# Value-stationary attention products in four column tiles, block transposes for their results, earlier requests for the last weights, no barrier behind the projections, and a redone order of units

## Chip, cores and metric

One core of one Trainium2 chip. The metric is device time in microseconds (us) for one execution; lower is better.

Terms: PE is TensorE, which multiplies matrices; DVE is VectorE, ACT is ScalarE, POOL is GpSimd. TensorE writes its results to PSUM, which this kernel uses in eight banks; an eviction is the copy of a result out of PSUM by DVE or ACT, after which the bank is free again. Filler is work that no waiting step needs at once, put where TensorE would idle.

## The reference, cut to what matters

The result is `g * a + (1 - g) * b`, with two independent attentions over one input of 2048 rows by 512 columns.

**A** is recurrent. The 2048 rows are 64 segments of 32 rows. Each segment gets 8 memory rows in front, and those are the first 8 output rows of the segment before:

```python
for s in range(n_seg):                       # 64, strictly one after another
    h = concatenate([mem, xs], axis=1)       # 8 + 32 rows of 512
    q, k, v = h @ Wq, h @ Wk, h @ Wv         # 32 heads of 128
    p = softmax(mask(q @ k.T * scale))
    o = (p @ v) @ Wo                         # 40 rows of 512
    mem = o[:, :M, :]                        # needed by the next segment
    outs.append(o[:, M:, :])
```

**B** is a causal attention in 4 blocks of 512 rows, 32 heads of 16, with a linear-attention memory carried from block to block. Its softmax-weighted values are divided by their sum, scaled by `1 - g`, and from the second block on a memory part `(phi(q) @ M) / (phi(q) @ z) * g` is added.

A is a loop of 64 dependent steps. B is independent of A, and the kernel uses it to fill TensorE's idle time between A's steps.

## The kernel before

Each engine gets a fixed list of operations; semaphore waits come from recorded reads and writes. A segment of A is a list of named units, one list for each segment number modulo 4. This is the second one:

```python
# K0x..V1y: projections of half 0/1 of the heads; k0,q0,v0: their evictions; TQ,TK: transposes
# S: scores, X: exp, M: row sums, L: reciprocal, N: normalise (n: the "left" columns)
# PV0/PL0, PV1/PL1: values times probabilities, main and left part, of half 0 and 1
# E0a,E0b,E1a,E1b: evictions of those;  W..: product with Wo;  H,l: split into high and low;  F: fold
# Fc,Ff,Fe: filler for the next four segments;  hm,ax: evictions of memory rows and of the other rows;  oL: left outputs set aside
#  bS,bE,bP: B's scores, exp, PV;  bT: B's result chain
"""Q0x K0x bE Q0y K0y K1x q0 TQ0 V0x Q1x Q1y k0 TK0 q1 S0 K1y X0 V0y TQ1 M0 k1 bS TK1 L0 bP V1x n0 S1 V1y X1 M1 Fc N0 bE v0 L1 v1
   PV0 PL0 Fc N1 E0b bP E0a Fe n1 Fe PV1 PL1 W0a W0b E1b E1a bT W1b W1a H0 H1 l0 bS l1 Ff bP F0 Ff oL hm0 ax0 F1 hm1 bE ax1 Fe Fe"""
A_ENG = dict(E0a="dve", E0b="act", ..., H0="act", Q0="dve", Q1="dve", ...)   # who evicts what
```

B's PV has the probabilities stationary and moves 17 columns (16 values and a one for the sum):

```python
for e, kc, q, col in blocks:
    for x in range(2):
        pe.matmul(pb[ob][:, o:o+17], pt[:, x, col:col+128], V[:, kc, 17*h:17*(h+1)], ...)
# chain: DVE reads the sums, takes reciprocals, multiplies; TensorE turns the result with 4 transposes
```

Before the segments lie B's projections, the loads of the weights, and a barrier:

```python
bar = []
for e in ("pe", "act", "dve", "gp"):
    o_ = P.ops[e][-1]; o_.post = True; bar.append(o_)
P.extra = bar
```

The softmax here doesn't subtract the row's maximum and nothing guards it: scores larger than these inputs give would overflow.

## Time and profile before

| | before |
|---|---|
| median, 3 runs (range) | 996.97 us (995.89 to 999.29) |
| profiled span | 994.1 us |
| TensorE / DVE / ACT busy | 93 % / 62 % / 58 % |
| end of segment 0 / of segment 63 | 107.0 / 985.6 us |
| mean segment | 13.95 us |

A segment's end is the end of the second copy of its memory rows (`hT`) out of PSUM.

**How segments are accounted below.** From the trace, from the end of segment 4 to the end of segment 56, I take the start-to-start time of every two neighbouring TensorE groups. A fixed time for each kind of group and 90 to 113 ns for each change of tile mode (the values that undisturbed neighbours show) count as work; the rest is waiting. Gaps inside a group count as waits "inside groups". Before, a segment of 14.10 us has 12.95 us work and 1.15 us waits. (The prediction has 12.4 and 1.7: it took the fast tenth of every pair of groups as work, which is stricter. I compare differences only.)

### The profile page before, as it was taken

How to read it: one execution, taken by the hardware profiler on the slowest of the kernel's cores; microseconds unless marked ns; L12 is line 12 of the kernel's file. 1: busy time of each engine (PE TensorE's matmuls, PEld its weight loads, DVE VectorE, ACT ScalarE, POOL GpSimd, SP SyncE). 2: the span in 40 equal slices, each digit the busy share in tenths (PEclk: the TensorE clock that was granted, in tenths of full speed). 3: DMA queues.
4: the chain of work that ended last, by engine and by line, in shares of the span. 5: the costliest groups of instructions: out<-in, count | busy, mean ns of one | idle time of the engine just before them, and what ended most of it. 6: DMA issues, size and time to landing. Idle time of an engine off the chain costs nothing.

```text
span 994.1 us, 57017 instructions
## 1 busy us (share of the span) xinstructions
PE 925.5 (93%) x25669; PEld 546.3 (55%) x25669; DVE 619.1 (62%) x1536; ACT 579.9 (58%) x1195; POOL 259.8 (26%) x672
## 2 busy tenths in 40 slices
PE   7986899999999999999999999999999999999986
PEld 4433455555555555555555555555556555555554
DVE  4664456666566666666665766666666667667664
ACT  4454456566666656656666566656656656665443
POOL 6201122222222222322232322232222222322110
PEclk9998899999999999999999999999999999999999
DMA  9897000000000111010001111010011101000010
GB/s 299 282 382 232 19 12 17 12 18 17 17 21 21 44 41 29 21 26 16 22 19 31 43 34 33 20 27 14 20 32 36 36 21 36 21 21 4 25 41 18
DMA packets 65899, 51.71 MB, mean 52 GB/s; under 512 B 34288, under 2 KB 64120, under 8 KB 64120
## 3 DMA queue, kind: packets, MB, share of 16 engines
q1 hardware_dynamic: 65656, 48.06, 16.5%
q8 instruction: 202, 3.31, 1.4%
q14 instruction: 41, 0.34, 0.1%
HBM read 33.47 MB, written 14.57 MB: 48 GB/s over the span
## 4 chain that ended last, share of the span: by engine, by line
PE 81%; ACT 6%; DVE 5%; DMA 3%; issue 3%; SPq 0%; ACTq 0%; POOL 0%; DVEq 0%; POOLq 0%
PE ps L890 40%; PE ps L943 14%; PE ps L716 4%; PE ps L769 3%; PE ps L964 3%; PE ps L591 2%; PE ps L1167 2%; PE ps L1111 2%; PE ps L1137 2%; PE ps L566 2%; DMA scr_pQd<-stgp 2%; PE ps L1104 1%; PE ps L1031 1%; DMA Wo_sb<-in_A_Wo_dram 1%; PE ps L1107 1%
## 5 line engine op out<-in xcount | busy, mean ns | idle before, releaser
L738 POOL TENSOR_SCALAR_AFFINE_SELECT PT<-PT 128x256 bf16<-128x256 bf16 (+1 forms) x224 | 98.3, 439 | 262.9 <-ACT PT L730 200.3
L730 ACT ACTIVATE PT<-ps 128x1024 bf16<-128x1024 f32 x160 | 163.1, 1020 | 5.6 <-PE ps L716 5.4
L320 ACT ACTIVATE KN_sb<-ps 128x512 bf16<-128x512 f32 x128 | 96.9, 757 | 101.3 <-PE ps L890 100.2
L890 PE MATMUL ps<-Wv_sb,hT 128*32 128x512 bf16 x2048 | 147.5, 380 | 0.3 <-ACT KN_sb L320 0.3
L943 PE MATMUL ps<-Wo_sb,OT_sb 128*32 128x256 bf16 x4096 | 139.2, 276 | 7.7 <-DMA Wo_sb<-in_A_Wo_dram 3.3
L890 PE MATMUL ps<-Wk_sb,hT 128*32 128x512 bf16 x2048 | 146.2, 382 | 0.1
L890 PE MATMUL ps<-Wq_sb,hT 128*32 128x512 bf16 x2048 | 142.2, 382 | 0.0
L322 DVE CAST QN_sb<-ps 128x512 bf16<-128x512 f32 x128 | 96.1, 751 | 62.5 <-PE ps L890 61.4
L943 PEld LDWEIGHTS ps<-Wo_sb,OT_sb 128*32 128x32 bf16 x4096 | 99.1, 97 | 26.0 <-issue 9.6
L1157 POOL TENSOR_TENSOR Pn_sb<-P_sb,R_sb 128x64 bf16<-128x64 bf16 x128 | 47.8, 373 | 233.8 <-ACT R_sb L1147 212.7
L902 DVE STREAM_TRANSPOSE KT_sb<-KN_sb 128x256 f32<-128x256 f32 x128 | 57.0, 446 | 65.5 <-ACT KN_sb L320 64.5
L322 DVE CAST V_sb<-ps 128x512 bf16<-128x512 f32 x128 | 87.1, 680 | 11.0 <-PE ps L890 10.2
L320 ACT ACTIVATE OT_sb<-ps 128x320 bf16<-128x320 f32 x192 | 76.2, 433 | 28.6 <-PE ps L1180 28.3
L1120 ACT ACTIVATE P_sb<-ps 128x224 bf16<-128x224 f32 x128 | 45.7, 357 | 76.5 <-PE ps L1111 64.7
L320 ACT ACTIVATE WH<-ps 128x256 bf16<-128x256 f32 x128 | 42.5, 381 | 76.3 <-PE ps L943 61.2
L954 DVE TENSOR_TENSOR WL<-ps,WH 128x256 bf16<-128x256 f32 x128 | 48.7, 420 | 52.8 <-ACT WH L320 45.8
L890 PEld LDWEIGHTS ps<-Wq_sb,hT 128*32 128x32 bf16 x2048 | 47.6, 96 | 53.0 <-DVE hT L322 12.2
L890 PEld LDWEIGHTS ps<-Wk_sb,hT 128*32 128x32 bf16 x2048 | 50.6, 96 | 43.3 <-ACT KN_sb L320 1.5
L320 ACT ACTIVATE LN_sb<-ps 128x512 bf16<-128x512 f32 (+1 forms) x80 | 46.2, 604 | 35.1 <-PE ps L890 18.7
L890 PEld LDWEIGHTS ps<-Wv_sb,hT 128*32 128x32 bf16 x2048 | 48.9, 96 | 30.1 <-ACT KN_sb L320 0.7
L769 PEld LDWEIGHTS ps<-Vj,PT 128*128 128x128 bf16 x1280 | 43.3, 96 | 35.9 <-issue 27.0
L716 PE MATMUL ps<-QTj,KTj 32*128 32x384 bf16 (+3 forms) x512 | 62.1, 301 | 0.1
(129 smaller groups left out, 1515.5 us busy)
## 6 DMA issues: line engine op xcount, KB each, us to landing
Wk_sb<-in_A_Wk_dram SPq DMA_DIRECT2D x4, 1024.0 KB, 6.9
Wq_sb<-in_A_Wq_dram SPq DMA_DIRECT2D x4, 1024.0 KB, 7.4
Wv_sb<-in_A_Wv_dram SPq DMA_DIRECT2D x4, 1024.0 KB, 9.2
Wo_sb<-in_A_Wo_dram SPq DMA_DIRECT2D x4, 1024.0 KB, 10.7
scr_vd<-V SPq DMA_DIRECT2D x16, 136.0 KB, 5.9
Vj<-scr_vd SPq DMA_DIRECT2D x32, 68.0 KB, 2.6
Wo_sb<-in_A_x_dram SPq DMA_DIRECT2D x4, 512.0 KB, 7.5
scr_kTd<-stgk SPq DMA_DIRECT2D x16, 128.0 KB, 6.6
```

What stands on the lines that cost most here:

```text
L320: P.op("act", lambda a: a.activation(dst, src, ACT.Copy), reads=[v.rbank[k] for k in bks], writes=dres, name=name)
L322: P.op("dve", lambda d: d.tensor_copy(dst, src), reads=[v.rbank[k] for k in bks], writes=dres, name=name)
L716: ins = pe.matmul(v.pb[bks[x]][:, o:o + w], KT[e][r, 128 * kc:128 * (kc + 1)], QT[r, q0:q0 + w], start=True, stop=True, tile_position=(r.s ...
L730: P.op("act", lambda a: a.activation(pt[:, :, :], v.ps[:, bks[0]:bks[1] + 1, :], ACT.Exp, scale=v.SCALE_B), reads=[v.rbank[b] for b in bks ...
L738: P.op("gp", lambda g, mv=mv: g.affine_select(mv, mv, [[0, mv.shape[1]], [1, 128]], ALU.is_ge, 0.0, base=0, channel_multiplier=-1), reads= ...
L769: ins = pe.matmul(v.pb[ob][:, o:o + 17], pt[:, x, col:col + 128], V[:, kc, 17 * h:17 * (h + 1)], start=first, stop=True, skip_group_check= ...
L890: ins = pe.matmul(pb[bk][SEG * j:SEG * (j + 1), :], lhs(c), cols(w, j) if split else w[:, 512 * j:512 * (j + 1)], start=(c == 0), stop=(c ...
L902: P.op("dve", lambda d: d.transpose(to, src), reads=reads, writes=writes, name=name)
L943: ins = pe.matmul(pb[bks[hf]][SEG * j:SEG * (j + 1), 0:HD], lhs(4 * k + j), Wo_sb[:, 4 * k + j, HD * hf:HD * (hf + 1)], start=(first and k ...
L954: P.op("dve", lambda d: d.tensor_tensor(lo[:, c], pb[bks[hf]][:, 0:HD], hi[:, c], ALU.subtract), reads=[rbank[bks[hf]], Rs(res[0][hf])], w ...
L1120: P.op("act", lambda a: a.activation(P_sb[:, b, :], pb[bk][:, 0:224], ACT.Exp, scale=SCALE), reads=[rbank[bk]], writes=[Rs("P%d" % b)], na ...
L1157: P.op(ENG["n"], lambda d: d.tensor_tensor(left(Pn_sb), left(P_sb), grp04(R_sb[:, b, :]), ALU.mult), reads=[Rs("P%d" % b), Rs("R%d" % b)], ...
```

## The change

Intent: take TensorE time out of B and out of the changes of tile mode, take the start's barrier away, and use ACT's spare time.

- B's PV has the values stationary, in four column tiles of 32, with 256 or 128 moving columns: 768 matmuls instead of 1280. Results come out transposed; DVE turns them with 32x32 block transposes (56 from PSUM, 16 of the joined result), and TensorE's 64 transposes go.
- B's chain and its memory part become two pieces. The unit orders and the engine choices are redone: Q0 of A goes from DVE to ACT, H0 from ACT to DVE.
- The barrier goes. Each tile that lies over memory of the projections waits for what used it. Wo is requested inside the projections.

```diff
-            for e, kc, q, col in blocks:
-                for x in range(2):
-                    ins = pe.matmul(v.pb[ob][:, o:o + 17], pt[:, x, col:col + 128], V[:, kc, 17 * h:17 * (h + 1)], ...)
+            for kc, q0, w, o in self.PIECES[k]:
+                for j in range(4):
+                    ins = pe.matmul(v.pb[ob][32 * j:32 * j + 32, q0:q0 + w], V[:, kc, G, 17 * j:17 * j + 32],
+                                    pt[:, j // 2, 256 * (j % 2) + o:256 * (j % 2) + o + w], start=(k == 0), stop=True, ...)
         if k == 4:
             self.late.append(lambda: self.chain(job, G, ob))
+            if sb:
+                self.late.append(lambda: self.memory(job, G))
+    def turned(self, bk, name):
+        P.op("dve", lambda d: d.transpose(v.oTt[:, :, :], src), reads=[v.rbank[bk]], writes=[Rs("oTt")], name=name)
...
-        if len(weights) > 4 and n % 5 == 0:
+        if weights and (n % 5 == 0 or n > 55 and n % 2):
             weights.pop(0)()
-    bar = []
-    for e in ("pe", "act", "dve", "gp"):
-        o_ = P.ops[e][-1]
-        o_.post = True
-        bar.append(o_)
-    P.extra = bar
...
     # the second of the four unit orders
-    Q0x K0x bE Q0y K0y K1x q0 TQ0 V0x Q1x Q1y k0 TK0 q1 S0 K1y X0 V0y TQ1 M0 k1 bS TK1 L0 bP V1x n0 S1 V1y X1 M1 Fc N0 bE v0 L1 v1 PV0 PL0
-    Fc N1 E0b bP E0a Fe n1 Fe PV1 PL1 W0a W0b E1b E1a bT W1b W1a H0 H1 l0 bS l1 Ff bP F0 Ff oL hm0 ax0 F1 hm1 bE ax1 Fe Fe""",
+    bS Fe K0x K0y Q0x Q0y K1x k0 bP Q1x Q1y TK0 K1y q0 TQ0 bE S0 q1 k1 V0x bS TQ1 TK1 V0y V1x S1 X0 bE V1y X1 M0 v0 L0 M1 L1 n0 v1 Fc bP
+    Ff N0 PV0 PL0 N1 E0a Fe PV1 n1 bT PL1 E0b E1a W0a E1b oL W0b W1a W1b H1 bP bS H0 Fc Ff l0 l1 F0 hm0 ax0 bE F1 hm1 Fe ax1 Ff Fe""",
-A_ENG = dict(..., H0="act", KL0="dve", Q0="dve", VL0="dve", ...)
+A_ENG = dict(..., H0="dve", KL0="act", Q0="act", VL0="act", ...)
```

A's probabilities are now normalised in place.

## The prediction

> **What bounds the kernel.** TensorE. The profile page gives PE 93% busy, 81% of the chain that ended last, DVE 62%, ACT 58%. The granted clock is 1.00 from 200 to 800 us. From the end of one segment's memory rows to the next it takes 14.1 us (mean of segments 5 to 55; timeline, the 128x16 casts to hT). Adding start-to-start times of matmul groups (their fast tenth as base) over 200 to 900 us, about 12.4 us of a segment is work and about 1.7 us waits, spread over many places (Wo to fold, V projection, second PV half). Before the segments lies a start of 79 us: projections end at 70.6, the first segment projection starts at 79.2 (barrier; POOL xL), then PE waits for Wo (landed about 101.8); segment 0 ends at 107.
>
> **What changes on PE.** B's PV takes 1280 matmuls of 17 columns, 25 to 28 ns each: about 33 us. [...] After: 768 matmuls in four column tiles, 640 of 256 columns and 128 of 128. The Wo matmuls have that shape and take 28 ns each (111 ns for four), so estimated 18 us: saves 15.
>
> Tile shape changes cost too. [...] Here eight projection matmuls take 432 ns before another column-tiled group and 553 before B's PV; score pieces take 320 instead of 216. Each switch thus costs about 0.09 to 0.12 us. Counting both programs' PE order I find about 743 switches before, 616 after: saves 12 to 13 us. The 64 result transposes (3.6 us) go to DVE; the memory products grow from 3.4 to 5.2. Scores stay (same columns). Sum: about 28 us less PE work, 0.45 us a segment.
>
> **Other engines.** DVE gains 56 block transposes, estimated 0.7 us each (128x64 takes 0.25, 128x256 0.45): 40 us; it loses Q0 (48 us) and two left evictions (22), gets H0 (27): about level. ACT gains about 45 us and stays under 67%. POOL loses about 20 us of masks. None becomes the bound.
>
> **Start.** Without the barrier the first segment projection needs only xL (over V17, whose last stores land about 73) and weights: I expect it near 73 to 75. Wo requested inside the projections should land near 90 instead of 102. Segment 0 should end near 96: 8 to 13 us gained. All of it is on the critical path.
>
> **How much is realised.** Where PE is latency-bound, less filler means longer waits: the last segments, with roughly 2.5 us less work, get only 1.6 us shorter (12.5 against 14.1). So I count 65 to 105% of 28 us (the order was redone): 18 to 30, plus 8 to 13 at the start. Predicted 958 us, range 941 to 974; faster by over 2%: 0.91, within: 0.08, slower: 0.01.
>
> **What would show it.** B's PV groups of four at about 110 ns with no gain in time of the projection before; segments near 13.6 us; first segment projection at 73 to 75; no PE wait for Wo above 1 us; PE busy under 900 us; DVE about 620, ACT about 625.
>
> **What would make it wrong.** DVE in order: a block transpose plus its chain (about 1.6 us) before H0 holds up the fold, so waits grow over 2 us a segment. Wo's 4 MB ahead of the last stores delays stage buffers that lie under the segment's tiles. Or the new order removes more waits than I credit, and the time falls under 941.

B's matmuls of 17 columns start 25 ns apart (median). About 28 us less TensorE work, 0.45 us a segment, rests on the times that stand beside it (25 to 28 ns for a matmul of 17 columns, 28 ns for one of Wo's, 432 ns against 553 and 216 against 320 for a change of tile shape).

## More of the kernel before

The two halves of the heads interleave: while half 0 goes through its softmax (S0, X0, M0, L0, N0), TensorE projects half 1 (K1, V1). Each half of PV takes four of the eight PSUM banks:

```python
def pv_main(b):
    bks = held[b] = B.pair() + B.pair()          # four banks
    for i in range(4):
        for j in range(4):                       # 16 matmuls, one bank per 32 rows
            pe.matmul(pb[bks[j]][:, L*i:L*(i+1)], V_sb[...], Pn_sb[...], tile_position=(SEG*j, 0), ...)
# ... ot_ev(b, half): one eviction per two banks, on DVE or ACT, gives them back
```

The profile page of the kernel before: the busy time of each engine with its instruction count, the queue that carries instructions, and the chain of work that ended last.

```profile
PE 925.5 (93%) x25669; PEld 546.3 (55%) x25669; DVE 619.1 (62%) x1536; ACT 579.9 (58%) x1195; POOL 259.8 (26%) x672
...
q8 instruction: 202, 3.31, 1.4%
...
PE 81%; ACT 6%; DVE 5%; DMA 3%; issue 3%; SPq 0%; ACTq 0%; POOL 0%; DVEq 0%; POOLq 0%
```

TensorE is the bound: 81 % of the chain. The second line says 202 packets and 3.31 MB of instructions, that is 16.4 KB each.

The groups of TensorE instructions of the kernel before, by shape: line, operation, output<-inputs, tile mode and shape, count, busy us and mean ns, then TensorE's idle time just before them and what ended it. They are the product with Wo, the PV of A and the fold.

```profile
L943 PE MATMUL ps<-Wo_sb,OT_sb 128*32 128x256 bf16 x4096 | 139.2, 276 | 7.7 <-DMA Wo_sb<-in_A_Wo_dram 3.3 <-issue 3.2 <-DVE LN_sb L954 0.7
...
L1167 PE MATMUL ps<-Pn_sb,V_sb 32*128 32x40 bf16 x2048 | 35.3, 178 | 14.8 <-ACT OT_sb L320 8.8 <-DVE OT_sb L322 2.8 <-DVE Pn_sb L1151 1.9
...
L964 PE MATMUL ps<-fold,WH 128*128 128x32 bf16 x256 | 29.3, 177 | 12.7 <-DVE WL L954 11.3 <-issue 0.3
```

The waits are small and spread. "issue" is time in which TensorE waited for nothing that the profile shows.

The timeline of TensorE in one segment of the kernel before, from the row sums of the second half to the product with Wo (start us, duration us, instruction group, count; in brackets the idle time before it, where there is a notable one).

```profile
449.57 0.28 PE L1137 MATMUL ps<-P_sb,onesb 128*32 128x160 bf16 x8
449.67 1.04 PE L890 MATMUL ps<-Wq_sb,xL 128*32 128x512 bf16 x16
450.64 0.27 PE L1167 MATMUL ps<-Pn_sb,V_sb 32*128 32x40 bf16 x16
450.76 0.25 PE L1180 MATMUL ps<-Pn_sb,VL 32*128 32x16 bf16 x16
450.94 1.05 PE L890 MATMUL ps<-Wq_sb,xL 128*32 128x512 bf16 x16
451.92 0.36 PE L769 MATMUL ps<-Vj,PT 128*128 128x17 bf16 x8
452.21 0.28 PE L1167 MATMUL ps<-Pn_sb,V_sb 32*128 32x40 bf16 x16
452.33 0.25 PE L1180 MATMUL ps<-Pn_sb,VL 32*128 32x16 bf16 x16
452.51 1.89 PE L943 MATMUL ps<-Wo_sb,OT_sb 128*32 128x256 bf16 x56
```

Between the two PV halves (L1167 and L1180 twice) stand 16 projection matmuls and a piece of B: TensorE has work while the first half is evicted.

## The result, and the profile after

| | before | after |
|---|---|---|
| median of 4 runs (range) | 996.65 us (995.89 to 999.29) | 1011.03 us (1010.03 to 1012.09) |
| ratio, fast runs | | 1.0140 [1.0117, 1.0163] |
| profiled span | 994.1 us | 1008.3 us |
| end of segment 0 | 107.0 us | 105.8 us |
| mean segment (1 to 63) | 13.95 us | 14.19 us |
| work / waits for each of segments 5 to 56 | 12.95 / 1.15 us | 12.43 / 1.80 us |

A ratio here is the mean time of one kernel's fast runs over the mean of the other's fast runs of the same rounds, so it is not quite the ratio of the medians quoted.

The change made the kernel 1.4 % slower; I had predicted 3.9 % faster. The spans differ by 14.2 us: 1.2 us won by the end of segment 0, and 63 segments of 0.25 us more each. Of those 15.6 us, 8.7 lie in segments 5 to 56, 4.1 in segments 1 to 4 and 2.8 in the last seven; only the 52 in the middle are taken apart below.

The same three parts of the page, after.

```profile
PE 908.5 (90%) x25349; PEld 536.3 (53%) x25349; DVE 624.9 (62%) x1558; ACT 628.0 (62%) x1227; POOL 250.9 (25%) x554
...
q8 instruction: 199, 3.26, 1.4%
...
PE 14%; ACT 1%; issue 1%; DVE 1%; POOL 0%; ACTq 0%; DVEq 0%
```

TensorE is less busy and idles more. DVE and ACT are where the prediction put them (620 and 625). The chain of waits adds up to 17 % only, so it broke off early and cannot be read here; I read waits group by group instead.

The same groups of TensorE after.

```profile
L959 PE MATMUL ps<-Wo_sb,OT_sb 128*32 128x256 bf16 x4096 | 132.2, 278 | 15.1 <-issue 13.9 <-ACT t_sb L1053 1.1
...
L1183 PE MATMUL ps<-P_sb,V_sb 32*128 32x40 bf16 x2048 | 38.0, 178 | 47.7 <-DVE OT_sb L356 31.7 <-ACT OT_sb L354 11.6 <-DVE P_sb L1167 3.3
...
L980 PE MATMUL ps<-fold,WH 128*128 128x32 bf16 x256 | 24.3, 180 | 2.0 <-DVE WL L970 1.6
```

Three things changed. The fold no longer waits for WL (1.6 us against 11.3), so the danger that I had named first did not come. PV waits 47.7 us instead of 14.8, nearly all of it for the evictions `OT_sb` of the other half. And the product with Wo waits 13.9 us for "issue", against 3.2.

The timeline of TensorE in one segment after, the same stretch as shown of before.

```profile
455.08 0.58 PE L1153 MATMUL ps<-P_sb,onesb 128*32 128x160 bf16 x16
455.48 1.04 PE L903 MATMUL ps<-Wq_sb,xL 128*32 128x512 bf16 x16
456.35 0.28 PE L788 MATMUL ps<-PT,Vj 128*32 128x128 bf16 x8
456.58 0.28 PE L1183 MATMUL ps<-P_sb,V_sb 32*128 32x40 bf16 x16
456.69 0.26 PE L1196 MATMUL ps<-P_sb,VL 32*128 32x16 bf16 x16
457.79 0.28 PE L1183 MATMUL ps<-P_sb,V_sb 32*128 32x40 bf16 x16 [0.85 <-ACT OT_sb L354]
457.90 0.26 PE L1196 MATMUL ps<-P_sb,VL 32*128 32x16 bf16 x16
458.09 1.60 PE L959 MATMUL ps<-Wo_sb,OT_sb 128*32 128x256 bf16 x52
```

Nothing stands between the halves any more. The second half must wait until the four banks of the first are evicted: 0.85 us idle. This is so in 51 of the 64 segments (in the others a piece of an output product stands there); in the kernel before it was so in 15, most of them of the third order.

The timeline of DVE in the same stretch: the normalisation of each half (L1167) and its eviction of half 0.

```profile
456.11 0.33 DVE L1167 TENSOR_TENSOR P_sb<-P_sb,R_sb 128x160 bf16<-128x160 bf16 x1
456.67 0.33 DVE L1167 TENSOR_TENSOR P_sb<-P_sb,R_sb 128x160 bf16<-128x160 bf16 x1 [0.24 <-PE ps L788]
457.16 0.49 DVE L356 CAST OT_sb<-ps 128x320 bf16<-128x320 f32 x1 [0.16 <-POOL P_sb L1173]
```

And of ACT, its eviction of half 0.

```profile
457.23 0.43 ACT L354 ACTIVATE OT_sb<-ps 128x320 bf16<-128x320 f32 x1
```

Both halves of PV start on a latency and not when TensorE is free. PV0 starts at 456.58, 0.14 us after the first normalisation ends (456.44). PV1 starts at 457.79, 0.13 us after the second eviction ends (457.66), though its own probabilities were ready at 457.00. Over segments 12 to 59 this repeats: in three of the four orders the time from the end of the first normalisation to PV0 has a median of 146 to 147 ns and a tenth percentile of 145 or 146, so PV0 is nearly always released by it. In the kernel before the medians of the same time are 0.55 to 2.0 us by order: there PV0 stood in a queue of other work and waited for nothing.

The timeline of TensorE at one of the "issue" waits after.

```profile
257.83 0.28 PE L959 MATMUL ps<-Wo_sb,OTL 128*32 128x256 bf16 x4
257.94 1.36 PE L959 MATMUL ps<-Wo_sb,OT_sb 128*32 128x256 bf16 x41
260.66 0.83 PE L959 MATMUL ps<-Wo_sb,OT_sb 128*32 128x256 bf16 x23 [1.36 <-issue]
```

TensorE stops in the middle of a run of 64 matmuls, all of whose operands were there, for 1.36 us by this view (1.53 us from start to start beyond the usual step). I numbered TensorE's instructions (two for each matmul, plus those of its sequencer, such as semaphore waits). After, these are 51,089 (25,349 matmuls, as many weight loads, 391 others), and the instruction queue moved 199 packets of 16 KB: 257 instructions for each. Before, it is 51,733 for 202 packets, 256 each. From these counts I estimate that a packet is a block of 256 TensorE instructions. After, from 150 us on, there are 38 gaps of over 0.25 us inside groups; in 29 of them TensorE resumes at an instruction whose number modulo 256 is 192 or 193, and in those it resumes 1.22 to 1.59 us after a 16 KB packet of the instruction queue landed. These gaps look like TensorE waiting for its next block. The blocks at which it did not stop say the same: over 178 blocks of this trace, TensorE ran the instruction just before number 192 within 1.2 us of a landing in 27, but number 192 itself in none, the least time being 1.22 us; the traces of before, x6, x13, x14 and x18 have 1.21 to 1.25 us. Why the place is number 192 was not shown.

The accounting by kind (us for each of segments 5 to 56; sums can be off by some 0.04 us from gaps below the limits). "Instruction stalls" are the gaps inside groups that lie over 0.2 us beyond the step and end 1.15 to 1.70 us after such a packet; they are part of the column before.

| | work | all waits | between PV halves | before the fold | inside groups | instruction stalls |
|---|---|---|---|---|---|---|
| before | 12.95 | 1.15 | 0.16 | 0.20 | 0.27 | 0.13 |
| after | 12.43 | 1.80 | 0.77 | 0.04 | 0.57 | 0.43 |

So work fell by 0.52 us, a little more than predicted (0.45), and waits rose by 0.65: 0.61 between the halves and 0.30 by instruction stalls, less some 0.26 saved elsewhere, most of it at the fold. What has to be found out: which part of the change did this, whether the "issue" gaps are the instruction blocks, and whether either can be had back.

### The profile page after: what moved, and what is told of

It is laid out like the page before. It is cut to its first block, busy times and chain, and to the rows that moved or that the text cites. A ratio compares the mean times of both kernels' runs of the same rounds, so it can differ in the third digit from the quotient of the medians.

```text
span 1008.3 us, 56287 instructions
## 1 busy us (share of the span) xinstructions
PE 908.5 (90%) x25349; PEld 536.3 (53%) x25349; DVE 624.9 (62%) x1558; ACT 628.0 (62%) x1227; POOL 250.9 (25%) x554
## 3 DMA queue, kind: packets, MB, share of 16 engines
HBM read 33.47 MB, written 14.57 MB: 48 GB/s over the span
## 5 line engine op out<-in xcount | busy, mean ns | idle before, releaser
L959 PE MATMUL ps<-Wo_sb,OT_sb 128*32 128x256 bf16 x4096 | 132.2, 278 | 15.1 <-issue 13.9
L762 POOL TENSOR_SCALAR_AFFINE_SELECT PT<-PT 128x512 bf16<-128x512 bf16 (+1 forms) x96 | 75.8, 790 | 278.3 <-ACT PT L755 277.0
L903 PE MATMUL ps<-Wq_sb,hT 128*32 128x512 bf16 x2048 | 130.7, 381 | 0.0
L1173 POOL TENSOR_TENSOR P_sb<-P_sb,R_sb 128x64 bf16<-128x64 bf16 x128 | 55.5, 433 | 204.0 <-ACT R_sb L1163 164.6
L1183 PE MATMUL ps<-P_sb,V_sb 32*128 32x40 bf16 x2048 | 38.0, 178 | 47.7 <-DVE OT_sb L356 31.7
L354 ACT ACTIVATE WH<-ps 128x256 bf16<-128x256 f32 x64 | 24.6, 384 | 83.7 <-PE ps L959 81.4
L915 DVE STREAM_TRANSPOSE QT_sb<-QN_sb 128x256 f32<-128x256 f32 x128 | 56.9, 445 | 24.9 <-ACT QN_sb L354 22.5
L354 ACT ACTIVATE LN_sb<-ps 128x512 bf16<-128x512 f32 (+1 forms) x96 | 55.3, 576 | 24.3 <-PE ps L903 12.8
L356 DVE CAST WH<-ps 128x256 bf16<-128x256 f32 x64 | 27.1, 424 | 64.7 <-PE ps L959 64.4
L741 PE MATMUL ps<-QTj,KTj 32*128 32x256 bf16 (+1 forms) x768 | 64.0, 255 | 2.7 <-issue 2.5
L1183 PEld LDWEIGHTS ps<-P_sb,V_sb 32*128 32x128 bf16 x2048 | 25.5, 91 | 73.5 <-ACT OT_sb L354 52.0
```

Source lines behind the costliest of these rows:

```text
L354: P.op("act", lambda a: a.activation(dst, src, ACT.Copy), reads=[v.rbank[k] for k in bks], writes=dres, name=name)
L356: P.op("dve", lambda d: d.tensor_copy(dst, src), reads=[v.rbank[k] for k in bks], writes=dres, name=name)
L741: ins = pe.matmul(v.pb[bks[x]][:, 256 * e + o:256 * e + o + w], KT[e][r, 128 * kc:128 * (kc + 1)], QT[r, q0:q0 + w], start=True, stop=True ...
L762: P.op("gp", lambda g: g.affine_select(mv, mv, [[0, mv.shape[1]], [1, 128]], ALU.is_ge, 0.0, base=0, channel_multiplier=-1), reads=[rp], w ...
L903: ins = pe.matmul(pb[bk][SEG * j:SEG * (j + 1), :], lhs(c), cols(w, j) if split else w[:, 512 * j:512 * (j + 1)], start=(c == 0), stop=(c ...
L915: P.op("dve", lambda d: d.transpose(to, src), reads=reads, writes=writes, name=name)
```

## The experiments

The columns from "segment" on are us for each of the segments 5 to 56, as above. All results were correct. Each median is of 4 runs; the kernel before ran in the same rounds each time (medians 994.8 to 998.6 us). Line numbers differ by a few lines between variants.

| run | median us (range) | ratio to before [95 %] | segment | work | waits | PV halves | fold | instruction stalls |
|---|---|---|---|---|---|---|---|---|
| x1_oldsched | 1016.6 (1015.4 to 1021.6) | 1.0187 [1.0145, 1.0228] | 14.51 | 12.54 | 1.96 | 0.19 | 0.65 | 0.13 |
| x2_oldorder | 1055.2 (1053.2 to 1056.7) | 1.0562 [1.0526, 1.0598] | 15.12 | 12.54 | 2.58 | 0.24 | 0.74 | 0.18 |
| x3_oldeng | 1022.6 (1021.3 to 1024.4) | 1.0233 [1.0192, 1.0274] | 14.42 | 12.42 | 2.01 | 0.89 | 0.12 | 0.31 |
| x4_oldstart | 1017.1 (1012.3 to 1019.6) | 1.0176 [1.0133, 1.0219] | 14.25 | 12.38 | 1.83 | 0.77 | 0.04 | 0.41 |
| x6_shift | 993.5 (989.7 to 994.2) | 0.9948 [0.9923, 0.9974] | 14.01 | 12.43 | 1.54 | 0.78 | 0.01 | 0.30 |
| x7_bt | 1045.7 (1044.5 to 1046.8) | 1.0479 [1.0459, 1.0499] | 14.62 | 12.60 | 2.01 | 0.19 | 0.22 | 0.18 |
| x7_bt13 | 1011.2 (1009.5 to 1016.8) | 1.0145 [1.0103, 1.0186] | 14.26 | 12.60 | 1.66 | 0.19 | 0.32 | 0.17 |
| x8_fc | 1011.7 (1010.9 to 1013.8) | 1.0142 [1.0121, 1.0163] | 14.31 | 12.51 | 1.76 | 0.50 | 0.04 | 0.25 |
| x9_banks | 1009.4 (1002.4 to 1013.1) | 1.0107 [1.0054, 1.0159] | 14.32 | 12.38 | 1.90 | 0.77 | 0.05 | 0.44 |
| x10_phase | 991.5 (989.7 to 995.4) | 0.9941 [0.9908, 0.9973] | 14.06 | 12.38 | 1.65 | 0.78 | 0.02 | 0.31 |
| x11_before_banks | 996.9 (993.1 to 998.9) | 0.9985 [0.9951, 1.0019] | 14.07 | 12.90 | 1.16 | 0.16 | 0.21 | 0.11 |
| x12_before_phase | 994.5 (993.0 to 995.0) | 0.9967 [0.9940, 0.9994] | 14.05 | 12.90 | 1.15 | 0.16 | 0.20 | 0.09 |
| x13_shift256 | 1007.0 (1002.4 to 1009.8) | 1.0114 [1.0075, 1.0153] | 14.20 | 12.43 | 1.74 | 0.77 | 0.04 | 0.38 |
| x14_shift64 | 992.6 (990.2 to 995.0) | 0.9982 [0.9943, 1.0020] | 14.04 | 12.43 | 1.58 | 0.77 | 0.02 | 0.29 |
| x16_old_gap | 994.2 (993.9 to 1001.3) | 1.0007 [0.9965, 1.0049] | 13.99 | 12.62 | 1.37 | 0.15 | 0.18 | 0.05 |
| x17_old_gap2 | 1001.4 (1000.8 to 1002.2) | 1.0062 [1.0036, 1.0089] | 14.12 | 12.60 | 1.52 | 0.19 | 0.16 | 0.08 |
| x18_xl | 991.9 (985.4 to 996.9) | 0.9975 [0.9932, 1.0018] | 14.01 | 12.43 | 1.54 | 0.78 | 0.02 | 0.27 |

### First batch: which part of the change?

**x1_oldsched**: the new B and start with the order, engines and filler rule of the kernel before. Its order has too few slots for five late pieces, so chain and memory run as one.

```diff
-            if len(pend) > (mode == "c"):
+            if len(pend) > 1:
-            self.late.append(lambda: self.chain(job, G, ob))
-            if sb:
-                self.late.append(lambda: self.memory(job, G))
+            self.late.append(lambda: (self.chain(job, G, ob), self.memory(job, G) if sb else None))
+    (A_ORDER and A_ENG of the kernel before)
```

> The changed kernel with the unit order, the engine assignment, the filler rule and the one-piece chain of the kernel before; the new value product, block transposes, in-place probabilities and start stay. Theory A (the new unit order leaves nothing between the two halves of the segment's own value product, where TensorE waits 35 us in 700 against 12 before): the wait there falls back to about 0.25 us a segment, segments to about 13.6 us, time 960 to 975. Theory B (the engine assignment costs it): also 960 to 975, but then the third run shows it too and the second does not. Theory C (the block transposes and the longer DVE chain, or the in-place probabilities, cost it): stays at 1000 or more.

Measured: 1016.6 us. The idea that the new order alone was at fault fell. The wait between the halves is gone (0.19 us) and the instruction stalls are few (0.13), yet the fold waits 0.65 us. The group of the fold in x1_oldsched:

```profile
L979 PE MATMUL ps<-fold,WH 128*128 128x32 bf16 x256 | 30.6, 180 | 36.8 <-DVE WL L969 34.9 <-ACT VL L354 0.4
```

DVE makes WL late. In the first 16 segments, which have no memory part yet, the medians of the four orders are 13.4 to 13.7 us; in segments 16 to 56 they are 15.3 and 15.4 us for the first and second order (number modulo 4 = 0 or 1), 14.7 and 13.7 for the others. In the long ones DVE runs two block transposes and two chains, about 3.3 us in one piece, just ahead of WL. This is the danger the prediction named, and the new order was made to avoid it. All the gains that I had expected of this run were missed; only the range of theory C (1000 us or more) held.

**x2_oldorder**: as x1_oldsched, with the engine choices of the kernel after.

> As the first run, but with the new engine assignment (Q0 on ACT, H0 on DVE, left evictions on ACT). Theory A: within 8 us of the first run, 960 to 980. Theory B: 995 to 1010. Theory C: 1000 or more.

Measured: 1055.2 us, the slowest of all and far from theory A's 960 to 980. A segment waits 2.58 us. The new engine choices do not fit the old order.

**x3_oldeng**: the kernel after with the engine choices of before.

```diff
-A_ENG = dict(..., H0="dve", KL0="act", Q0="act", VL0="act", ...)
+A_ENG = dict(..., H0="act", KL0="dve", Q0="dve", VL0="dve", ...)
```

> The changed kernel with its new unit order, but the engine assignment of the kernel before. Theory A: 1000 to 1025, since the order is left and was made for the other assignment; the wait between the halves stays near 0.7 us a segment. Theory B: 965 to 985.

Measured: 1022.6 us. The engine choices are not at fault either; they are worth about 10 us to the new order.

**x4_oldstart**: the kernel after with the barrier, the loads and the places of the weight requests of before.

> The changed kernel with the start of the kernel before: barrier, loads of B's first job and the last weight requests behind the projections. If the new start is what costs (segments 1 to 3 took 44.1 us in the changed kernel against 39.5 before): 1003 to 1006. If the new start gains the little that the trace shows (segment 0 ends 1.2 us earlier): 1011 to 1016. In both cases segments stay near 14.2 us, as neither theory puts the main loss here.

Measured: 1017.1 us, and segment 0 ends at 111.2 instead of 105.8 us. That the new start helps, by some 5 us, is likely but not clear of noise: the intervals of the two ratios overlap (1.0133 to 1.0219, and 1.0117 to 1.0163 for the kernel after), and this trace has the granted clock at 0.5 for 10.2 us from 99.9 us on, where the kernel after has it for 3.4. The segments are those of the kernel after (14.25 us against 14.27). So the loss lies in the segments.

### Second batch: the instruction blocks, DVE's place, and filler between the halves

**x6_shift**: 64 unneeded matmuls, 128 TensorE instructions, between projections and segments, where TensorE is idle (from 74.3 to 81.3 us in the kernel after).

```diff
+    bk = v.BK.take()
+    def idle(pe):
+        for i in range(64):
+            ins = pe.matmul(v.pb[bk][:, 0:16], v.ident[:, :], v.ident[:, 0:16], start=True, stop=True)
+        return ins
+    P.op("pe", idle, reads=[v.Rs("ident")], writes=[v.rbank[bk]], name="idle")
+    v.BK.give(bk)
     v.home = late_home
     plan_a(v, NSEG_RUN)
```

> The kernel after, with 64 small unneeded matmuls (two TensorE instructions each, 128 in all, half a block of 256) between the projections and the segments, in a stretch where TensorE waits anyway. Results unchanged. Theory F (TensorE's instructions come in blocks of 256, and in some segments the next block is late): every stall inside a group ends again at the same place in a block, but that is now another group of the segment, so the slow segments (in the kernel after 7-11, 19-23, 31-35 ...) move by about 5 segments, while the total stays within 5 us of the kernel after (1006 to 1016 us). Rival D (those stalls come from data or from B's loads, bound to the program's work): the same segments are slow at the same places of their groups. A total below 1000 us would say that the position of the blocks alone decides.

Measured: 993.5 us, 17 us less than the kernel after, for doing more work. I had expected the slow segments to move and the sum to stay, so half of this expectation missed. 22 of 24 stalls again end at the 192nd or 193rd instruction of a block, and only one of them is at a place in the program where the kernel after has one. But the run did two things: taking and giving a PSUM bank also changes every later choice of banks. The third batch separates the two.

**x7_bt**: x1_oldsched with chain and memory as two pieces, taken at the start of each segment, and one more in the fourth order.

```diff
-    Q0x K0x bE Q0y ... PV1 PL1 W0a W0b E1b E1a bT W1b W1a ...
+    bT Q0x K0x bE Q0y ... PV1 PL1 W0a W0b E1b E1a W1b W1a ...
```

> The kernel after with the unit order, engine choice and filler rule of the kernel before, chain and memory part kept as two pieces, and the pieces taken at the start of each segment (in the fourth order also at its old place) instead of between Wo and the fold. Theory C (in the run x1_oldsched the vector engine's chain of about 3.3 us in one piece ahead of WL held up the fold: fold waits 0.66 us per segment, segments 15.3 us where it ran in one piece, 13.4 to 13.7 in the first 16, which have no memory part): the fold waits fall under 0.3 us, segments near 13.6 us, total 970 to 985 us, faster than both kernels. Rival (it is the amount of vector work, not its place): the waits go elsewhere, to the scores and M0/M1 behind the evictions of Q and K, total 1005 to 1020.

Measured: 1045.7 us, a miss of over 60 us. The fold's wait did fall to 0.22 us, but there were too few slots for the pieces, which ran late, and B's loads hang on them. TensorE's waits by cause in x7_bt (total us, times, longest):

```profile
PE ps L788 <- DMA MZj<-scr_mzd: 13.4, 5, 3.5
PE ps L1043 <- DMA oTg<-scr_oTd: 12.7, 3, 4.3
```

Two DMA waits of 26 us together are new. The run says little about DVE's place.

**x7_bt13**: one more slot, at the old place in the second order.

> As x7_bt, with the piece also at its old place in the second order, so that the fourth order's second place is rarely needed. Theory C: within 4 us of x7_bt. If a block transpose behind the second Wo half holds up the fold again, segments of the second kind (numbers 1, 5, 9 ...) are over 0.5 us longer than in x7_bt, and the total about 8 us longer.

Measured: 1011.2 us. It is 34 us faster than x7_bt, which shows the missing slots, and its second-order segments (median 14.57 us) are 0.8 us longer than its third (13.79): there the late piece stands ahead of WL. The fourth order, with such a slot too, has 14.57 as well.

**x8_fc**: one filler piece of 16 projection matmuls moved between the halves, in the first and the fourth order (the other two find no bank).

```diff
-    ... V1y M0 M1 Fc L0 bP bP Ff v0 v1 L1 N0 N1 n0 PV0 PL0 E0a n1 Fe Ff E0b PV1 ...
+    ... V1y M0 M1 L0 bP bP Ff v0 v1 L1 N0 N1 n0 PV0 PL0 Fc E0a n1 Fe Ff E0b PV1 ...
```

> The kernel after with one unit moved in the first and the fourth order: the filler piece Fc that stood ahead of PV0 now stands between PL0 and PV1, where TensorE waits 0.75 to 0.9 us for the eviction of the first half. Theory H (that wait is what the new order costs, and filler there is worth its length): the wait between the halves falls by 0.4 us or more in these segments (half of all), nothing else grows, total 998 to 1004. Rival (the first half of the softmax is then late instead: without Fc ahead of PV0, PV0 waits for N0): the wait moves to the place before PV0, total within 5 us of the kernel after.

Measured: 1011.7 us, unchanged. One such segment:

```profile
444.51 0.28 PE L1179 MATMUL ps<-P_sb,V_sb 32*128 32x40 bf16 x16 [0.77 <-DVE P_sb L1163]
444.62 0.26 PE L1192 MATMUL ps<-P_sb,VL 32*128 32x16 bf16 x16
444.81 1.05 PE L899 MATMUL ps<-Wk_sb,xL 128*32 128x512 bf16 x16
446.62 0.27 PE L1179 MATMUL ps<-P_sb,V_sb 32*128 32x40 bf16 x16 [0.76 <-ACT LN_sb L354]
```

The filler has left the place ahead of PV0, and PV0 now waits 0.77 us for the normalisation. And PV1 still waits, now for the filler's own eviction on ACT (`LN_sb`), which runs ahead of that of PV0. Over all segments the wait between the halves fell by 0.27 us, and that before PV0 rose by 0.45 (0.05 to 0.50). The move also shifted the instructions within their blocks, and the stalls fell by 0.18 (0.43 to 0.25), so by itself it rather cost time. The rival holds: in the new order the stretch from the sums to Wo is a chain of latencies, and filler can only choose which of them it covers.

### Third batch: blocks or banks?

**x9_banks**: the bank taken and given back, without any instruction (`v.BK.give(v.BK.take())` before the segments).

> The run x6_shift came out 17 us faster than the kernel after, but it did two things: it moved TensorE's instructions by 128 within their blocks, and, because a PSUM bank was taken and given back, it changed the order in which banks are handed out from there on (816 of the 1266 later choices differ). This run does the second alone: the kernel after with one bank taken and given back before the segments, not one instruction more. Theory P (which bank a piece gets, and so whose eviction it waits for, is what the kernel after lost by): 990 to 997 us, as x6_shift, waits inside groups near 0.40 us per segment. Theory F (the place in the instruction blocks): 1007 to 1015 us, as the kernel after.

Measured: 1009.4 us. The banks are not it.

**x10_phase**: the 64 unneeded matmuls in a bank that is free anyway, so that all later banks are those of the kernel after (`bk = v.BK.free[0]`, nothing taken).

> The other half of x6_shift alone: the kernel after with the same 64 unneeded matmuls in the idle start, written to a bank that is free then, without taking it, so all later banks are those of the kernel after. Theory F: 990 to 997 us. Theory P: 1007 to 1015 us. If it lies half way, both play a part.

Measured: 991.5 us, 19.5 us less than the kernel after. The group of the product with Wo in x10_phase:

```profile
L967 PE MATMUL ps<-Wo_sb,OT_sb 128*32 128x256 bf16 x4096 | 132.8, 281 | 11.1 <-issue 9.8 <-ACT t_sb L1061 1.3
```

"issue" fell from 13.9 to 9.8 us in this group alone, and the run of 64 matmuls that stopped for 1.36 us at 260 us in the kernel after runs through here.

**x11_before_banks** and **x12_before_phase**: the same two edits on the kernel before.

> The kernel before with one bank taken and given back before the segments, no instruction more (about all later bank choices differ). Theory P says that the kernel before, which was tuned with its own bank order, can only lose or stay: 997 to 1015 us. Theory F: 994 to 1000 us.

> The kernel before with the 64 unneeded matmuls between projections and segments, banks unchanged. Theory F: the kernel before has few instruction stalls (0.13 us per segment, against 0.46 after), so its place may be a lucky one: up to 15 us longer, and never below 990. Theory P: 995 to 1000 us, no change.

Measured: 996.9 and 994.5 us, ratios 0.9985 and 0.9967. The kernel before hardly minds either. It was not tuned to a lucky place: its order just has few stalls at both places (0.09 to 0.13 us).

### Fourth batch: a whole block, and DVE's place again

**x13_shift256**: 128 unneeded matmuls, a whole block.

> As x10_phase (banks of the kernel after), but 128 unneeded matmuls, 256 TensorE instructions: every later instruction is one whole block further on, at the same place in its block as in the kernel after. Theory F (the place in the block decides): back to 1006 to 1016 us, and the stalls inside groups fall on the same segments as in the kernel after (0.46 us per segment). Rival T (the unneeded matmuls help in another way, for instance by keeping TensorE busy or by delaying the first segment): 985 to 996 us, as x10_phase.

Measured: 1007.0 us; a whole block takes the gain back. The same run of matmuls as shown above of the kernel after stops again, at an earlier time since this run is some 6 us ahead there:

```profile
251.73 1.35 PE L967 MATMUL ps<-Wo_sb,OT_sb 128*32 128x256 bf16 x38
254.17 0.83 PE L967 MATMUL ps<-Wo_sb,OT_sb 128*32 128x256 bf16 x23 [1.09 <-issue]
```

**x14_shift64**: 32 unneeded matmuls, a quarter of a block.

> As x10_phase with 32 unneeded matmuls, a shift of 64 instructions, a quarter of a block. Theory F: another set of segments is hit; between 988 and 1016 us, stalls still end at the 192nd to 193rd instruction of a block and 1.2 to 1.6 us after a packet has landed. Rival T: 993 to 1003, half way, with the stalls where they are in the kernel after.

Measured: 992.6 us. Comparing the places of the stalls (by the number of semaphore instructions that TensorE had run before, which names a place in the program whatever the time), from 90 us on:

| run | shift, instructions | stalls | at a place where the kernel after stalls |
|---|---|---|---|
| after | 0 | 33 | 33 |
| x9_banks | 0 | 31 | 30 |
| x13_shift256 | 256 | 27 | 27 |
| x14_shift64 | 64 | 20 | 9 |
| x10_phase | 128 | 19 | 2 |

That settles it. A whole block gives the same places; half a block gives others. In x13_shift256 all 27, and in x14_shift64 19 of 20, end at the 192nd or 193rd instruction of a block. (In x9_banks and x10_phase matmul records are missing from the trace (22 of 25,413 in x10_phase), so the count drifts and cannot be read; their places can.)

**x16_old_gap**: x7_bt with the pieces just ahead of PV1 in every order, and at the start of the first and third. By then DVE has done its eviction and is idle for 2.3 us until WL, and the memory product fits the wait between the halves.

```diff
-    ... PV0 PL0 Fc N1 E0b bP E0a Fe n1 Fe PV1 PL1 W0a W0b E1b E1a bT W1b W1a ...
+    ... PV0 PL0 Fc N1 E0b bP E0a Fe n1 Fe bT PV1 PL1 W0a W0b E1b E1a W1b W1a ...
```

> The kernel after with the unit order, engines and filler rule of before, chain and memory part as two pieces, taken just ahead of PV1 in each order (DVE has done N1 and its eviction by then and idles 2.3 us until WL; the memory product of 0.85 us fits the wait of TensorE between the halves) and at the start of the first and third. Theory C (DVE's place ahead of WL is what cost x1_oldsched and x7_bt13): waits of fold under 0.15 us per segment (0.57 and 0.35 in those), the segments 13.4 to 13.7 us, total 965 to 985 us. If the vector engine's amount of work matters and not its place: 1000 to 1020 us, as the other placements.

Measured: 994.2 us, equal to the kernel before. TensorE's waits by cause in x16_old_gap:

```profile
PE ps L976 <- DVE WL L966: 12.3, 25, 0.8
...
PE ps L955 <- DVE oTt L802: 5.5, 9, 0.7
...
PE ps L1179 <- DVE oTt L802: 4.1, 5, 0.8
```

The place matters: 22 us less than x1_oldsched, with the fold's wait on WL back where the kernel before has it (12.3 us against 11.3). But it falls short of my 965 to 985: the block transposes (L802) now hold up the second PV half and Wo, 9.6 us together, and DVE is at 660 us of busy time. In this order both place and amount matter.

**x17_old_gap2**: the pieces at the start of every segment, and ahead of PV1 in the second and fourth order only.

> As x16_old_gap with the pieces at the start of every segment and ahead of PV1 in the second and fourth order only. Theory C: within 8 us of x16_old_gap, and at least 20 us under x7_bt13 (1011.15), which differs only in where the second and fourth order take their second piece (there between E1a and the second Wo half, ahead of WL). Otherwise 1000 to 1015 us.

Measured: 1001.4 us, 10 us under x7_bt13 instead of the 20 that I had expected. Same direction, half the size.

### Last run: the start

**x18_xl**: x10_phase with the small tile xL over the weights of B's K projections, which are used up early.

```diff
-    in_a = alloc(esA, ("LN_sb", ...), ..., ("VL", [128, 2, 512], BF16, 2), ("xL", [128, C, SEG], BF16, 0), ...
+    in_a = alloc(esA, ("xL", [128, C, SEG], BF16, 0), ("LN_sb", ...), ..., ("VL", [128, 2, 512], BF16, 2), ...
```

> x10_phase with the small tile xL laid over the weights of B's K projections, which are used up early, instead of over V17, so its copy need not wait for V17's last store (landed 80.8 us in x10_phase, where the copy ran at 80.9 and the first segment projection at 81.3). My prediction took this wait for the start's bound. Theory W (Wo's landing at about 98 us bounds the start, since the first Wo product waits for it): the first segment projection moves to 75 to 79 us, the first Wo product and the end of segment 0 (99.1 and 102.9 in x10_phase) stay within 1.5 us, total 987 to 994 us. Theory X (xL's wait bounds it): segment 0 ends 4 to 6 us earlier, total 984 to 988 us.

Measured: the first segment projection starts at 75.9 us instead of 81.3, and segment 0 ends at 103.3 instead of 102.9. The first Wo product starts at 98.1 us instead of 99.1, just after Wo's last quarter landed (97.9). Theory W holds: Wo bounds the start. The total, 991.9 us, is that of x10_phase.

Why Wo came late, in windows of the start (stretch in us, length, busy time and count of PE, PEld, DVE, ACT and POOL, granted clock, busy share of the DMA engines, GB/s), first before, then after:

```profile
60.00:75.00 15.00, 10.56 (x49) 4.61 (x47) 8.85 (x18) 7.33 (x12) 0.00 (x0) 1.00 1.05 402
75.00:90.00 15.00, 10.78 (x164) 4.95 (x168) 5.59 (x11) 5.23 (x7) 1.93 (x6) 0.77 0.53 152
```

```profile
60.00:75.00 15.00, 14.15 (x67) 6.09 (x64) 8.48 (x17) 6.51 (x11) 0.00 (x0) 1.00 0.96 311
75.00:90.00 15.00, 8.74 (x105) 3.75 (x108) 5.73 (x13) 6.08 (x10) 0.59 (x2) 0.66 1.06 390
```

Before, the DMA engines are half idle from 75 to 90 us; the change fills that gap (share 1.06, 390 GB/s). But up to 75 us they now move less, and they are busy throughout from 60 to 90 us. Wo was requested from 77.5 us on instead of 85.9, Wv's last part landed at 83.5 instead of 76.5, and Wo's last quarter at 98.5 instead of 101.8.

## Why the prediction was wrong, point by point

- **TensorE work: right.** 0.45 us less for each segment predicted, 0.52 measured (12.95 to 12.43), although the mix of B's PV was miscounted: the trace has 512 matmuls of 256 columns and 256 of 128, not 640 and 128. B's PV in column tiles takes 109 ns for a group of four between column-tiled groups. A change of tile mode costs about 0.1 us here (the accounting takes 90 to 113 ns; neighbours in the two traces lie between 80 and 130 ns), and these changes fell from 1.24 to 1.04 us for each segment.
- **DVE's chain holds up the fold by over 2 us: did not happen.** The fold's waits fell to 0.04 us. The danger was real, as x1_oldsched shows (0.65 us), but the new order avoids it, and pays elsewhere.
- **"65 to 105 % realised" of 28 us: this is the step that failed.** I took waits as roughly constant, scaled down a little where TensorE is latency-bound. They rose by 0.65 us for each segment, more than the work fell, so nothing was realised. Two terms were missing.
  - *Between the PV halves, +0.61 us, about 39 us over 64 segments.* The second half waits for the eviction of the first, with nothing in between. I had read the new order only for the place of B's pieces, not for what it leaves between PL0 and PV1. x8_fc shows that filler there is no gain by itself: it leaves a wait at least as long ahead of PV0. In the new order both halves pass through the softmax together behind all projections, so that nothing covers these latencies. It is the order and not the work that TensorE lost: x1_oldsched has lost the same work and waits 0.19 us here.
  - *Instruction blocks, +0.30 us, about 19 us.* I left them out. The kernel after loses 0.38 to 0.44 us for each segment at its place in the blocks (after, x9_banks, x13_shift256) and 0.27 to 0.31 at others (x6_shift, x10_phase, x14_shift64, x18_xl); a shift of half a block is worth 19.5 us of median, not all of it in stalls that I can count (see below). All nine kernels with A's old order lose 0.05 to 0.18. So the new order is prone to it, and the place decides how much.
- **Start, 8 to 13 us: 1.2 us in this pair of traces.** Traces of one start differ: segment 0 ends at 102.2 to 109.3 us in six with the order and start of the kernel after (after, x6, x9, x10, x13, x14) and at 107.0 to 110.0 in three of the kernel before, so the gain is 4.4 us between the medians (102.9 against 107.3), and segment 0 never ended near the 96 us predicted. The term was mis-sized because I expected Wo to land near 90 us; it landed at 98.5, while the DMA engines were full (share 0.96 and 1.06 from 60 to 90 us). The other wait I had counted, that of xL, is worth at most 1 us (x18_xl). Also, the granted clock fell to 0.5 at 36.0 us for 6.8 us in the trace of the kernel after, and the projections ended 3.7 us later than before (74.3 against 70.6). Such a dip near 36 us stands in 12 of the 15 traces with the new start and in 1 of the 4 with the old one (x11_before_banks). So the new start may well have a part in it; no run tested that.
- **Old-order reading.** The rival "the order was at fault, the old one would be good" fell: x1_oldsched is no better. The old order with the new B reaches the kernel before at best (x16_old_gap, 994.2 us). With the place moved, the new order does slightly better than before, by 0.2 to 0.6 % (x10_phase 0.9941, x6_shift 0.9948, x18_xl 0.9975, x14_shift64 0.9982; the intervals of the last two include 1).

What stays open. Why the next block comes too late at some borders and not at others was not shown. No two packets start under 3.2 us apart in the traces of before and after, so my guess is that a run of very short matmuls uses up a block faster than the next one arrives; no run tested that by itself. Of the 20 us between the kernel after and x10_phase, 11 lie in segments 5 to 56, and the stalls as counted here explain 6 of those; the rest lies in the start, the first and the last segments, and I did not take it apart. And no run could take away the wait between the halves alone, so that its worth in isolation is an inference from x8_fc and the timelines.

## What to carry to other kernels

Work taken off a bound engine can be worth nothing where the engine then waits for a chain of latencies (here 0.52 us less work and 0.65 us more waits for each segment): before predicting a gain, list for every dependent pair of steps what stands between them in the new order, and how long the step between takes. When TensorE stops in the middle of a run of instructions with "issue" as the cause, number its instructions; if the stops share a place modulo 256 (29 of 38 did in the kernel after), shift the program by half a block before judging the change. A one-line edit that should do nothing, such as that shift or x9_banks, measures how far a result depends on accident: here 20 us for one order and 2 to 3 us for the other.
